# Weight loads moved from SP's queue to GpSimd's, and one split's low part made two turns later

## The chip, the cores and the metric

The kernel runs on one core of a Trainium2 chip. The time is the device time of one execution in microseconds. Three runs of the kernel before took 670.84, 672.91 and 673.17 us; the median is 672.91.

The engines that matter: PE (TensorE) multiplies matrices, DVE (VectorE) and ACT (ScalarE) work on elements, POOL (GpSimd) does a little set-up, and SP (SyncE) issues the DMAs. Each engine has a queue of its own that it works through in order. A DMA instruction in a queue waits there until its semaphores allow it, and what stands behind it waits too.

## The reference

Windowed attention with sink tokens, and then two MLPs, all in float32:

```
scores = q k^T / 8,   kept where key < 4 or 0 <= query - key < 128
x = softmax(scores) v                     (2 batches, 8 heads, 768 tokens, head size 64)
h = x @ w_in ;  g = max(h, 0) + alpha * min(h, 0) ;  y = g @ w_out    (1536 x 512, 512 x 2048)
h = y @ w2_in ; g = h - tanh(h) ;                    out = g @ w2_out
```

The weights arrive as 64-bit floats. [...]

## The kernel before

**Attention** goes in turns `n`, one for a pair of heads of one block of 128 tokens (96 turns; four make a block `u`). A turn's work on DVE is the mask and maximum (`s_max`, L279), the sum and its reciprocal (L294, L296), the scaling of the probabilities (`norm`, L303), and sometimes a copy of the sink columns (L309) and the differences that split a float into a high and a low part (`kq_lo` L237, `x_l` L374). PE makes the scores of the next turn (`s_mm`, L264 for the first block, L270 later), transposes the scaled probabilities (L319) and multiplies them by v (L358 to L362).

**The MLPs** go in 96 steps `g`: twice three groups of 512 tokens, each over 16 slices `f` of 128 hidden units. Every float32 operand of these matmuls is split into a high part of fewer bits and the remainder; three products are summed. `split_w` makes the high part of a weight tile on ACT (`wh`, L215), `split_lo` the low part on DVE (`wl`, L220). Part 0 of a slice feeds `h_mm` (L389), part 1 feeds `out_mm` (L441).

**Weights** come slice by slice. `load_w` (L194) issues two DMAs of 512 KB, L197 and L198, into one of two staging buffers. `conv_w` turns them into floats: two ACT instructions (L73, L74) and two DVE instructions (L76, L78), spread over steps. L78 is the last that reads the staging buffer, so the load of slice f+2 waits for L78 of slice f. There are 32 loads, 16 for each MLP.

**The order** is written out by hand: the program order of each engine is the order in which the Python code names its instructions (`manual_schedule`). The opening runs 19 turns (S_LEAD) of attention alone, `n` from 0 to 18, with the conversion of slice 0 begun in turn 8 and of slice 1 in turn 12 (CONV0). From then on each step of the first MLP carries one attention turn, until the turns are used up. During the first MLP's first token group each step also converts one slice of the first MLP's weights. The second MLP's weights are converted from the end of the second token group on.

SP issues nearly everything: the q and k loads (L180, four DMAs of 64 KB for each half block), v (L185), the sink rows (L188), the weights (L197, L198) and the results. In the opening POOL makes two iotas (L491, L492) and the identity matrix, and after that it has nothing to do. The masks of the attention are built by DVE from the iotas (L494 to L503).

The place that the change touches in the opening loop stands at the end of a turn, behind the conversions' own steps:

```
            for f, at in CONV0:                      # (0, 8), (1, 12)
                ...
                if at < n < at + 5:
                    conv_step(0, f)
                ...
                if n == at + 6 and f == 0:           # turn 14
                    split_w(0, 0, 0, 0)              # ACT, L215
                    split_lo(0, 0, 0, 0)             # DVE, L220
```

In turn 14 the loop comes to f = 0 first and to f = 1 after it, so the split of slice 0 stands ahead of L78 of slice 1 in DVE's queue.

Of the kernel before, what the change touches and what calls it, by code (L numbers as in the profile page):

```python
# [11 lines left out]
I32 = mybir.dt.int32  # L12
# [68 lines left out]
def load_scalars(nc, pool, limits):  # L81

    raw = pool.tile([128, 2, 2], I32, name="ns_raw")
    nc.sync.dma_start(out=raw.rearrange("p a t -> p (a t)"), in_=limits.bitcast(I32).partition_broadcast(128))
    val = pool.tile([128, 2], F32, name="ns_val")
    return raw, val
# [52 lines left out]
def fast_path(tc, qk, v, vsink, limits, w1i, w1o, alpha, w2i, w2o, out, outer):  # L139
    nc = tc.nc  # L140
    keep = outer.enter_context(tc.tile_pool(name="keep", bufs=1))
    bad_i = keep.tile([1, 1], I32, name="bad_i")
    with ExitStack() as ctx:
# [50 lines left out]
        def load_w(m, f):  # L194
            wi, wo = ((w1i, w1o), (w2i, w2o))[m]
            raw = stage[m][f % 2]
            nc.sync.dma_start(out=raw[:, 0:1024], in_=wi[f].rearrange("p k c -> p (k c)").bitcast(I32))  # L197
            nc.sync.dma_start(out=raw[:, 1024:2048], in_=wo[f * 128:(f + 1) * 128, :].bitcast(I32))  # L198

        def conv_w(m, f):  # L200
            raw = stage[m][f % 2]
# [9 lines left out]
        def split_w(m, c, f, part):  # L211
            src = wf[m, f][:, 512 * part:512 * part + 512]
            hi = wp.tile([128, 512], F32R, name=f"wh{part}", tag=f"wh{part}", bufs=2)
            lo = wp.tile([128, 512], F32R, name=f"wl{part}", tag=f"wl{part}", bufs=2)
            nc.scalar.activation(out=hi, in_=src, func=AF.Copy, scale=W_DOWN)  # L215
            whl[m, c, f, part] = (hi, lo)

        def split_lo(m, c, f, part):
            hi, lo = whl[m, c, f, part]
            nc.vector.scalar_tensor_tensor(lo, wf[m, f][:, 512 * part:512 * part + 512], W_DOWN, hi, op0=ALU.mult, op1=ALU.subtract)  # L220
# [34 lines left out]
        def s_mm(n):  # L255

            u, p, b, i, w = geom(n)
            for a in range(2):
                if (n, a) not in sps:
                    sps[n, a] = ps_tile(["o"] if initial[0] else ["st"[a]])  # L260
            if u == 0:
                for a in range(2):
                    t = raws[2 * u + p // 2][64 * a:64 * a + 64, p % 2]
                    nc.tensor.matmul(sps[n, a][:, :w], lhsT=t[:, 0, :], rhs=t[:, 1, :], start=True, stop=True)  # L264
                return
            at = 0 if u % 2 == 0 else K_ODD + 128
            for e, (l, r) in enumerate(((0, 0), (1, 0), (0, 1))):
                for a in range(2):
                    h = slice(64 * a, 64 * a + 64)
                    nc.tensor.matmul(sps[n, a][:, :w], lhsT=kq[l][h, p, at:at + 128], rhs=kq[r][h, p, K_EVEN:K_EVEN + w], start=e == 0, stop=e == 2)  # L270

        def s_max(n, a):
            u, p, b, i, w = geom(n)
            G, hh = 2 * u + p // 2, 2 * (p % 2) + a
            if hh == 0:
                pq[G] = ap.tile([128, 4, 288], F32, name="pq", bufs=2)
                sums[G] = ap.tile([128, 4], F32, name="sums", bufs=2)
            mask = m_zero if i == 0 else m_one if i == 1 else m_even if i % 2 == 0 else m_odd
            nc.vector.tensor_tensor_reduce(  # L279
                out=pq[G][:, hh, 0:w], in0=sps.pop((n, a))[:, :w], in1=mask[:, 0:w], scale=-0.125, scalar=BIG,  # L280
                op0=ALU.add, op1=ALU.min, accum_out=nm[:, 2 * n + a:2 * n + a + 1],
            )

        def s_exp(n, a):
            u, p, b, i, w = geom(n)
            G, hh = 2 * u + p // 2, 2 * (p % 2) + a
            e = pq[G][:, hh, 0:w]
            nc.scalar.activation(out=e, in_=e, func=AF.Exp, scale=-1.0, bias=nm[:, 2 * n + a:2 * n + a + 1], accum_out=sums[G][:, hh:hh + 1])  # L288

        def norm_sum(n, part):  # L290
            u, p, b, i, w = geom(n)
            r = sums[2 * u + p // 2][:, 2 * (p % 2):2 * (p % 2) + 2]
            if part == 0:
                nc.vector.tensor_scalar(r, r, 1e-9, None, op0=ALU.add)  # L294
            else:
                nc.vector.reciprocal(r, r)  # L296

        def norm(n):
            u, p, b, i, w = geom(n)
            G, hh = 2 * u + p // 2, 2 * (p % 2)  # L300
            for a in range(2):
                e = pq[G][:, hh + a, 0:w]
                nc.vector.tensor_scalar(e, e, sums[G][:, hh + a:hh + a + 1], None, op0=ALU.mult)  # L303
        def sink_copy(n):
            u, p, b, i, w = geom(n)
            G = 2 * u + p // 2
            if p % 2 == 1 and i >= 2:
                sks[G] = ap.tile([128, 4, SINK], F32, name="sk", bufs=1)
                nc.vector.tensor_copy(sks[G], pq[G][:, :, 128:160])  # L309

        def t_mm(n):
            u, p, b, i, w = geom(n)
            G, hh = 2 * u + p // 2, 2 * (p % 2)
            tps[n] = t = ps_tile(["t", "h"] if initial[0] else ["t"])
            cur = 0 if i % 2 == 0 else 160
            for a in range(2):
                for e, c in ((0, 160 - cur), (1, cur)):
                    if i > 0 or e == 1:
                        nc.tensor.transpose(t[:, 256 * a + 128 * e:256 * a + 128 * e + 128], pq[G][:, hh + a, c:c + 128], ident)  # L319

        def t_ev(n):
            u, p, b, i, w = geom(n)
            ptb[n] = ap.tile([128, 2, 2, 128], F32, name="pt", bufs=2)
            e0 = 1 if i == 0 else 0
            tv = tps.pop(n).rearrange("p (a e c) -> p a e c", a=2, e=2)
            nc.scalar.activation(out=ptb[n][:, :, e0:, :], in_=tv[:, :, e0:, :], func=AF.Copy)  # L326

        def has_sinks(n):
            u, p, b, i, w = geom(n)
            return p % 2 == 1 and i >= 2  # L330
# [12 lines left out]
        def sink_ev(n):  # L343
            pts[n // 2] = ap.tile([128, 128], F32, name="pts", bufs=2)
            nc.scalar.activation(out=pts[n // 2], in_=tps.pop((n, 0))[:, 384:512], func=AF.Copy)
# [123 lines left out]
        raw, val = load_scalars(nc, const, limits)  # L469
# [50 lines left out]
        def a_loads(n):  # L520

            u, p = divmod(n, 4)
            if p == 3 and 2 <= u + 1 < NU:
                load_v(u + 1)
            if n % 2 == 0 and 6 <= n // 2 + 4 < 2 * NU:
                load_qk(n // 2 + 4)
            if n == 4 * NB + 4:
                load_vs(1)


        def splits_hi(n):

            for G in {0: (0, 2), 1: (1,)}.get(n, (n // 2 + 2,) if n % 2 != (n < S_LEAD - 1) else ()):
                if G < 2 * NU:
                    kq_hi(G)
# [20 lines left out]
        for n in range(S_LEAD):  # L556
            last = n == S_LEAD - 1
            a_loads(n)
            if n == 0:
                s_mm(0)  # L560
            if not last:
                s_mm(n + 1)
            if n >= 2:
                t_ev(n - 2)
            s_max(n, 0)
            s_max(n, 1)
            s_exp(n, 0)
            s_exp(n, 1)
            if n >= 2 and has_sinks(n - 2):
                sink_ev(n - 2)  # L570
            if n >= 1:
                norm_sum(n - 1, 0)
                norm_sum(n - 1, 1)
                norm(n - 1)
                sink_copy(n - 1)
                if not last:
                    t_mm(n - 1)
                    if has_sinks(n - 1):
                        sink_mm(n - 1, n + 1)
            if n >= 2 and not last:  # L580
                pv(n - 2)
            splits_hi(n)
            if n >= 5 and n % 4 == 1:
                x_h(n - 2)
            splits_lo(n)
            if n >= 5 and n % 4 == 2:
                x_l(n - 3)
            if n == 1:
                masks(0)
            if n == 4:  # L590
                masks(1)
            if n == 3:
                load_w(0, 1)
            for f, at in CONV0:
                if n == at:
                    conv_start(0, f)
                if at < n < at + 5:
                    conv_step(0, f)
                if n == at + 4:
                    load_w(0, f + 2)  # L600
                if n == at + 6 and f == 0:
                    split_w(0, 0, 0, 0)
                    split_lo(0, 0, 0, 0)
        initial[0] = False
        conv_start(0, len(CONV0))
# [41 lines left out]
        for g in range(N):  # L647
            m, c, f = steps[g]
            n = S_LEAD + g
# [332 lines left out]
```

## Time and profile before

| | |
|---|---|
| median of 3 runs | 672.91 us |
| profiled execution, its own time | 672.6 us |
| its span in the profile | 670.8 us |
| PE busy | 640.8 us (96%), 3194 matmuls |
| DVE busy | 526.4 us (78%) |
| ACT busy | 472.5 us (70%) |
| POOL busy | 1.1 us, 8 instructions |
| mean DMA rate | 71 GB/s over the span |

The span runs from the first to the last instruction. Busy PE is matmuls in flight, whose ends are modelled. A row of the timeline gives the start in us, the duration (of a row that merges several instructions, the whole), the engine, the line of the kernel, the operation, the tiles (out<-in), and in brackets how long the engine had stood idle and what released it. `SPq` is SP's queue of DMA issues. The granted clock is a share of PE's full 2.4 GHz: 1.00 is that, 0.50 is 1.2 GHz.

### The profile page before, as it was taken

To read this page: it belongs to the slowest core of one execution; us is meant where nothing else is said; L and a number is where in the kernel's file an instruction comes from. 1 tells how busy PE (TensorE), PEld (TensorE's weight loads), DVE (VectorE), ACT (ScalarE), POOL (GpSimd) and SP (SyncE) were. 2 spreads that over 40 slices of the span, in tenths; PEclk is the share of its full clock that TensorE was granted. 3 is DMA by queue.
4 is the path that set the end of the run, shared out by engine and by line. 5 is a ranking of instruction groups with operands and counts; after the bars stand their busy time and mean duration, and the time that the engine had idled before them with its cause. 6 is when DMAs were issued, how large, how long until landed. Compare 5 with 4: busy or idle time off the path is not lost.

```text
span 670.8 us, 9201 instructions
## 1 busy us (share of the span) xinstructions
PE 640.8 (96%) x3194; PEld 504.2 (75%) x3194; DVE 526.4 (78%) x1098; ACT 472.5 (70%) x936; POOL 1.1 (0%) x8
## 2 busy tenths in 40 slices
PE   5886999999999999999899999999999999999996
PEld 3564677777777777777787887887888888888884
DVE  6877889799576665548877777889998888888883
ACT  5876888787566564557766757877877777777763
POOL 0000000000000000000000000000000000000000
PEclk9978899999999999999999999999999999999999
DMA  6543444463010000203343420100010000100001
GB/s 160 189 136 98 142 157 150 162 222 111 0 48 17 1 16 1 95 33 143 119 177 127 152 99 1 63 1 0 1 63 1 2 0 1 63 1 0 1 1 68
DMA packets 27032, 47.36 MB, mean 71 GB/s; under 512 B 3168, under 2 KB 15456, under 8 KB 26976
## 3 DMA queue, kind: packets, MB, share of 16 engines
q1 hardware_dynamic: 26400, 46.42, 20.0%
q8 instruction: 27, 0.44, 0.3%
q10 hardware_dynamic: 576, 0.26, 0.2%
q14 instruction: 29, 0.24, 0.1%
HBM read 43.53 MB, written 3.15 MB: 70 GB/s over the span
## 4 chain that ended last, share of the span: by engine, by line
PE 77%; ACT 8%; DVE 8%; issue 2%; DMA 2%; SPq 1%; ACTq 0%; DVEq 0%
PE ps_o L441 33%; PE ps_h L389 21%; PE ps_s L389 7%; PE ps_t L389 6%; ACT wf L73 2%; PE ps_t L319 2%; PE ps_s L270 2%; DMA raw<-in_moe_w_out_dram 2%; ACT raw L74 2%; PE ps_v L358 2%; PE ps_v L362 2%; PE ps_v L359 1%; PE ps_o L270 1%; DVE wf L78 1%; ACT pq L288 1%
## 5 line engine op out<-in xcount | busy, mean ns | idle before, releaser
L220 DVE SCALAR_TENSOR_TENSOR wl<-wf,wh 128x512 fp32r<-128x512 f32 x192 | 123.4, 683 | 44.7 <-ACT wh L215 44.7
L389 PE MATMUL ps_h<-x,wh 128*128 128x512 f32 x384 | 124.5, 405 | 2.1 <-ACT t L396 1.9
L215 ACT ACTIVATE wh<-wf 128x512 fp32r<-128x512 f32 x192 | 110.9, 628 | 5.1 <-PE ps_o L441 5.0
L389 PEld LDWEIGHTS ps_h<-x,wh 128*128 128x128 f32 x384 | 68.7, 189 | 18.2 <-ACT t L396 3.1
L441 PE MATMUL ps_o<-gh,wh 128*128 128x512 f32 x192 | 76.6, 399 | 0.3 <-DVE y L452 0.3
L389 PE MATMUL ps_h<-x,wl 128*128 128x512 f32 x192 | 75.8, 395 | 0.0
L441 PE MATMUL ps_o<-wh,gh 128*128 128x512 f32 x192 | 74.8, 390 | 0.2 <-ACT gh L420 0.2
L441 PE MATMUL ps_o<-gh,wl 128*128 128x512 f32 x192 | 74.9, 390 | 0.0
L441 PE MATMUL ps_o<-gl,wh 128*128 128x512 f32 x192 | 74.8, 390 | 0.0
L441 PE MATMUL ps_o<-wh,gl 128*128 128x512 f32 x192 | 74.8, 390 | 0.0
L441 PE MATMUL ps_o<-wl,gh 128*128 128x512 f32 x192 | 74.7, 389 | 0.0
L288 ACT ACTIVATE pq<-pq,nm 128x288 f32<-128x288 f32 (+1 forms) x96 | 48.4, 506 | 30.2 <-DVE nm L279 29.8
L420 ACT ACTIVATE gh<-g 128x512 fp32r<-128x512 f32 x48 | 30.4, 633 | 36.5 <-DVE g L127 36.5
L76 DVE SCALAR_TENSOR_TENSOR wf<-wf,raw 128x1024 int32<-128x1024 int32 x32 | 39.1, 1221 | 19.0 <-ACT raw L74 19.0
L326 ACT ACTIVATE pt<-ps_t 128x512 f32<-128x512 f32 (+1 forms) x39 | 21.9, 562 | 35.5 <-PE ps_t L319 35.4
L441 PEld LDWEIGHTS ps_o<-gh,wh 128*128 128x128 f32 x192 | 36.1, 188 | 9.2 <-issue 1.4
L420 ACT ACTIVATE gh<-t 128x512 fp32r<-128x512 f32 x48 | 30.1, 627 | 18.2 <-DVE t L408 18.2
L389 PEld LDWEIGHTS ps_h<-x,wl 128*128 128x128 f32 x192 | 36.2, 188 | 7.9
L441 PEld LDWEIGHTS ps_o<-wh,gh 128*128 128x128 f32 x192 | 36.0, 188 | 8.0 <-ACT gh L420 0.6
L441 PEld LDWEIGHTS ps_o<-wh,gl 128*128 128x128 f32 x192 | 36.0, 188 | 7.9 <-DVE gl L425 0.4
L441 PEld LDWEIGHTS ps_o<-gh,wl 128*128 128x128 f32 x192 | 36.0, 188 | 7.8
L73 ACT ACTIVATE wf<-raw 128x1024 f32<-128x1024 f32 x32 | 36.6, 1143 | 7.4 <-DMA raw<-in_moe_w_out_dram 7.3
(145 smaller groups left out, 1290.6 us busy)
## 6 DMA issues: line engine op xcount, KB each, us to landing
raw<-in_moe_w_in_dram SPq DMA_DIRECT2D x32, 512.0 KB, 3.3
raw<-in_moe_w_out_dram SPq DMA_DIRECT2D x32, 512.0 KB, 4.2
raw_qk<-in_qk_dram SPq DMA_DIRECT2D x92, 64.0 KB, 3.0
vt<-in_v_dram SPq DMA_DIRECT2D x12, 256.0 KB, 3.1
out_dram<-ob SPq DMA_DIRECT2D x2, 1024.0 KB, 4.2
out_dram<-ob SPq DMA_DIRECT2D x4, 256.0 KB, 3.4
vs<-in_vsink_dram SPq DMA_DIRECT2D x2, 256.0 KB, 3.6
raw_qk<-in_qk_dram ACTq DMA_DIRECT2D x4, 64.0 KB, 2.7
```

Of the source, the lines that this page charges most:

```text
L73: nc.scalar.activation(out=dst, in_=hw.bitcast(F32), func=AF.Abs, scale=W_UP, accum_out=seen)
L74: nc.scalar.activation(out=lw, in_=top, func=AF.Copy, scale=1.0 / 8192, bias=FLOOR)
L76: nc.vector.scalar_tensor_tensor(di, di, 3, lw, op0=ALU.logical_shift_left, op1=ALU.bitwise_or)
L215: nc.scalar.activation(out=hi, in_=src, func=AF.Copy, scale=W_DOWN)
L220: nc.vector.scalar_tensor_tensor(lo, wf[m, f][:, 512 * part:512 * part + 512], W_DOWN, hi, op0=ALU.mult, op1=ALU.subtract)
L270: nc.tensor.matmul(sps[n, a][:, :w], lhsT=kq[l][h, p, at:at + 128], rhs=kq[r][h, p, K_EVEN:K_EVEN + w], start=e == 0, stop=e == 2)
L288: nc.scalar.activation(out=e, in_=e, func=AF.Exp, scale=-1.0, bias=nm[:, 2 * n + a:2 * n + a + 1], accum_out=sums[G][:, hh:hh + 1])
L319: nc.tensor.transpose(t[:, 256 * a + 128 * e:256 * a + 128 * e + 128], pq[G][:, hh + a, c:c + 128], ident)
L326: nc.scalar.activation(out=ptb[n][:, :, e0:, :], in_=tv[:, :, e0:, :], func=AF.Copy)
L389: nc.tensor.matmul(h_ps[f], lhsT=l[:, w], rhs=x[:, r, kk, :], start=kk == 0 and e == 0, stop=kk == 3 and e == 2)
L420: nc.scalar.activation(out=gh, in_=mid[f], func=AF.Copy)
L441: nc.tensor.matmul(o, lhsT=l, rhs=r, start=f == 0 and e == 0, stop=f == NF - 1 and e == 2)
```

## The change

It has two parts. `load_w` issues both DMAs of each of the 32 loads on GpSimd's queue instead of SP's. And in the opening the low part of the first split (slice 0, part 0) is made at the end of turn 16, two turns behind its high part, which stays in turn 14.

```diff
             raw = stage[m][f % 2]
-            nc.sync.dma_start(out=raw[:, 0:1024], in_=wi[f].rearrange("p k c -> p (k c)").bitcast(I32))
-            nc.sync.dma_start(out=raw[:, 1024:2048], in_=wo[f * 128:(f + 1) * 128, :].bitcast(I32))
+            nc.gpsimd.dma_start(out=raw[:, 0:1024], in_=wi[f].rearrange("p k c -> p (k c)").bitcast(I32))
+            nc.gpsimd.dma_start(out=raw[:, 1024:2048], in_=wo[f * 128:(f + 1) * 128, :].bitcast(I32))
...
                 if n == at + 6 and f == 0:
                     split_w(0, 0, 0, 0)
+                if n == at + 8 and f == 0:
                     split_lo(0, 0, 0, 0)
```

On DVE, the end of turn 14 and the first maximum of turn 15 (`x` is the attention's output, `wl` the low part, `wf` a weight slice in conversion, `pq` the scores), before:

```order
L309 COPY sk<-pq 128x128
L374 TENSOR_TENSOR x<-ps_v,x 128x4x128
L220 SCALAR_TENSOR_TENSOR wl_649<-wf,wh_648 128x512
L78 SCALAR_TENSOR_TENSOR wf<-raw_90,wf 128x1024
L279 ISA pq,nm<-ps_o,m_odd 128x288
```

And the same place in the change, followed by the end of turn 16:

```order
L309 COPY sk<-pq 128x128
L374 TENSOR_TENSOR x<-ps_v,x 128x4x128
L78 SCALAR_TENSOR_TENSOR wf<-raw_90,wf 128x1024
L279 ISA pq,nm<-ps_o,m_odd 128x288
...
L303 TENSOR_SCALAR pq<-pq,sums 128x288 x2
L309 COPY sk<-pq 128x128
L220 SCALAR_TENSOR_TENSOR wl_649<-wf,wh_648 128x512
L279 ISA pq,nm<-ps_o,m_even 128x288
```

L220 has moved from ahead of L78 and the maxima of turn 15 to behind turn 16's copy of the sink columns and ahead of the maxima of turn 17.

On POOL, the start of the kernel, before:

```order
L977 UNCONDITIONAL_BRANCH
L491 ISA
L491 IOTA rel_i 128x128
L492 IOTA col_i 128x128
masks.py:197 MEMSET ident 128x128
masks.py:199 AFFINE_SELECT ident<-ident 128x128
L134 TENSOR_LOAD bad_i
```

And in the change:

```order
L978 UNCONDITIONAL_BRANCH
L197 DMA raw_90<-in_moe_w_in_dram 128x1024
L198 DMA raw_90<-in_moe_w_out_dram 128x1024
L491 ISA
L491 IOTA rel_i 128x128
L492 IOTA col_i 128x128
masks.py:197 MEMSET ident 128x128
masks.py:199 AFFINE_SELECT ident<-ident 128x128
L197 DMA raw_90<-in_moe_w_in_dram 128x1024
L198 DMA raw_90<-in_moe_w_out_dram 128x1024
```

The first load's two issues stand ahead of the iotas, the second's directly behind the identity matrix; the 30 other loads follow, with nothing between them.

On SP, the start of the kernel, before:

```order
L84 DMA ns_raw<-in_limits_dram 128x4
L180 DMA raw_qk<-in_qk_dram 64x2x128 x8
L185 DMA vt<-in_v_dram 128x512 x2
L180 DMA raw_qk<-in_qk_dram 64x2x128 x8
L188 DMA vs<-in_vsink_dram 128x512
L197 DMA raw_90<-in_moe_w_in_dram 128x1024
L198 DMA raw_90<-in_moe_w_out_dram 128x1024
L180 DMA raw_qk<-in_qk_dram 64x2x128 x4
L485 DMA al<-in_moe_alpha_dram 128x16
L197 DMA raw_90<-in_moe_w_in_dram 128x1024
L198 DMA raw_90<-in_moe_w_out_dram 128x1024
```

And in the change:

```order
L84 DMA ns_raw<-in_limits_dram 128x4
L180 DMA raw_qk<-in_qk_dram 64x2x128 x8
L185 DMA vt<-in_v_dram 128x512 x2
L180 DMA raw_qk<-in_qk_dram 64x2x128 x8
L188 DMA vs<-in_vsink_dram 128x512
L180 DMA raw_qk<-in_qk_dram 64x2x128 x4
L485 DMA al<-in_moe_alpha_dram 128x16
```

The weight loads are gone from SP's queue, and the rest keeps its order. PE's and ACT's instructions keep theirs.

## Rows read from the trace of the kernel before

**Rows 1.** Busy time by stretch: length, then PE, PEld, DVE, ACT, POOL, clock, DMA share, GB/s.

```profile
102.00:150.00 48.00, 47.14 (x256) 35.25 (x256) 42.63 (x100) 39.46 (x86) 0.00 (x0) 1.00 0.53 185
...
300.00:400.00 100.00, 97.78 (x435) 79.70 (x435) 77.48 (x102) 69.63 (x115) 0.00 (x0) 1.00 0.38 137
```

**Rows 2.** Timeline of turn 14: start, duration, engine, line, operation, idle time before and releaser.

```profile
48.97 0.66 PE L270 MATMUL ps_o<-kq 64*128 64x288 f32 x6
...
49.19 0.62 ACT L215 ACTIVATE wh<-wf 128x512 fp32r<-128x512 f32 x1
...
49.84 0.69 DVE L220 SCALAR_TENSOR_TENSOR wl<-wf,wh 128x512 fp32r<-128x512 f32 x1 [1.19 <-ACT wh L215]
...
50.45 1.22 DVE L78 SCALAR_TENSOR_TENSOR wf<-raw,wf 128x1024 int32<-128x1024 int32 x1
...
51.59 0.45 DVE L279 CUSTOM_DVE_ANT_0 pq<-ps_o,m_odd 128x288 f32<-128x288 f32 x1
...
53.25 0.82 PE L319 MATMUL ps_h<-ident,pq 128*128 128x128 f32 x4 [3.63 <-DVE pq L303]
```

**Rows 3.** Timeline of turn 16, PE's score matmuls and DVE's first maximum of turn 17.

```profile
56.22 0.98 PE L270 MATMUL ps_o<-kq 64*128 64x288 f32 x6
...
57.24 0.46 DVE L279 CUSTOM_DVE_ANT_0 pq<-ps_o,m_even 128x288 f32<-128x288 f32 x1 [1.28 <-PE ps_o L270]
```

**Rows 4.** Busy time by stretch, two microseconds within turns 15 and 16.

```profile
54.00:56.00 2.00, 2.00 (x13) 1.66 (x12) 1.86 (x9) 1.63 (x5) 0.00 (x0) 0.50 1.00 390
```

**Rows 5.** Waits of SP's own queue: total, times, longest.

```profile
SPq L197 <- DVE wf L78: 192.1, 28, 29.6
```

**Rows 6.** Weight loads: issue to landing of their tile, then from the page's DMA issues.

```profile
DMA to landing us min/median/max: 3.1/4.1/6.4
...
raw<-in_moe_w_out_dram SPq DMA_DIRECT2D x32, 512.0 KB, 4.2
```

**Rows 7.** Timeline: issues of weight loads on SP, and ACT's first reading of them.

```profile
78.41 0.43 SPq L198 DMA_DIRECT2D raw<-in_moe_w_out_dram  x1
...
83.13 1.14 ACT L73 ACTIVATE wf<-raw 128x1024 f32<-128x1024 f32 x1
...
122.12 1.16 ACT L73 ACTIVATE wf<-raw 128x1024 f32<-128x1024 f32 x1 [1.20 <-DMA raw<-in_moe_w_out_dram]
...
153.28 0.43 SPq L198 DMA_DIRECT2D raw<-in_moe_w_out_dram  x1
...
159.63 1.17 ACT L73 ACTIVATE wf<-raw 128x1024 f32<-128x1024 f32 x1
```

**Rows 8.** Timeline of PE: the first output matmul of four steps.

```profile
119.97 0.40 PE L441 MATMUL ps_o<-gh,wh 128*128 128x512 f32 x1
...
127.63 0.39 PE L441 MATMUL ps_o<-gh,wh 128*128 128x512 f32 x1
...
142.50 0.40 PE L441 MATMUL ps_o<-gh,wh 128*128 128x512 f32 x1
...
149.76 0.39 PE L441 MATMUL ps_o<-gh,wh 128*128 128x512 f32 x1
```

**Rows 9.** Timeline of the opening.

```profile
1.11 0.23 DVE L494 CAST rel<-rel_i 128x128 f32<-128x128 int32 x1
...
5.11 1.89 PE L264 MATMUL ps_o<-raw_qk 64*128 64x128 f32 x8 [5.11 <-DMA raw_qk<-in_qk_dram]
...
5.91 0.29 DVE L279 CUSTOM_DVE_ANT_0 pq<-ps_o,m_zero 128x128 f32<-128x128 f32 x1 [0.35 <-PE ps_o L264]
...
13.45 0.43 SPq L197 DMA_DIRECT2D raw<-in_moe_w_in_dram  x1
```

**Rows 10.** Busy time by stretch, two stretches of the opening.

```profile
2.00:4.00 2.00, 0.00 (x0) 0.00 (x0) 0.58 (x4) 0.23 (x2) 0.00 (x0) 1.00 0.72 118
...
16.00:18.00 2.00, 2.00 (x14) 1.23 (x12) 1.93 (x14) 1.72 (x7) 0.00 (x0) 1.00 1.00 398
```

**Rows 11.** Timeline of DVE, 0.3 us behind a conversion's last instruction.

```profile
115.96 0.48 DVE L303 TENSOR_SCALAR pq<-pq,sums 128x128 f32<-128x128 f32 x2
```

## The prediction

> **What bounds the kernel now.** I read the stretches first. In the first MLP's opening pass, where attention, weight conversion and matmuls run together, PE is busy 47.1 of 48 us, but DVE is busy 42.6 and ACT 39.5 [rows 1]: DVE has 11% of the stretch left, ACT 18%. There the work that feeds PE has little air. In the stretch from 300 us on, where the second MLP's weights are converted, PE is busy 97.8 of 100 us and DVE 77.5 [rows 1]: PE alone sets the pace. Second I read the timeline of the one place where the moved split stands, turn 14 [rows 2]; third, SP's own waits and the landings of the weight loads [rows 5 to 7]; last, the first microseconds [rows 9, 10].
>
> **Part 1, the low part two turns later.** In turn 14 DVE is free at 48.65 us but waits 1.19 us for ACT to finish the high part, then spends 0.61 us on the low part until the next instruction starts at 50.45, and only then comes L78 and, at 51.59, the score maximum of the next turn [rows 2]. PE meanwhile stands 3.63 us for the normalised scores that come behind this maximum [rows 2]. With the low part gone, L78 starts at 48.65, takes its 1.14 us (50.45 to 51.59), and the maximum can start at 49.79: the scores that it reads are written by PE at 48.97 + 0.66 = 49.63, so they are just there, and the next thing that would be late is nothing before 49.79. Gain 51.59 − 49.79 = 1.80 us, and PE's idle time falls from 3.63 to 1.83.
> What is put back two turns on costs 0.61 us of DVE. It stands between turn 16's copy of the sink columns and turn 17's first maximum, where DVE waits 1.28 us for PE's scores [rows 3]; 0.61 fits inside, and the high part is then long written, so there is no wait in it. If PE's scores came 0.7 us earlier there, the cover would be gone and 0.61 would count. The first user of the low part is the first MLP's first matmul, after turn 18. So I take −1.8, with bounds −1.2 (cover gone) and −3.1. The −3.1 is the clock: from 54 us on PE's granted clock is 0.50, which is the lower level, 1.2 GHz [rows 4], and the six score matmuls take 0.98 us there against 0.66 before the idle stretch [rows 2, 3]. Should the shorter idle stretch leave the clock at its upper level, the 3.95 us of PE between 53.25 and the maximum's start at 57.24 less its 0.04 shrink by a third, 1.3 us. I do not count it, since 1.83 us of idle time remain.
>
> **Part 2, the weight queue.** What it removes from SP: 64 issues of some 0.4 us (0.43 in the rows) and their waits. But the waits at L197 are for DVE's L78 in 28 of the 32 loads, 192.1 us in all [rows 5]: the queue waited because the staging buffer was still being read, and GpSimd's queue will wait for the same L78. No weight load can start earlier in the steady part. The q, k and v loads behind them on SP go earlier, yet no engine waits for one of those after the first at 5.11 us [rows 9]. So the gain is 0.
> What it adds: POOL issues instead of SP, and no row of this trace shows a POOL issue. The bounds for how much later a pair of loads lands: 0 (as on SP), and 2.3 us, the longest landing of a weight load less the median, 6.4 − 4.1 [rows 6]. I take 1.0, nearer the lower, because the 1.05 MB of a pair take 2.6 us at the 398 GB/s of a stretch with full engines [rows 10], and this part of a landing is the same for any issuer. The Trainium skill ("DMA: Bandwidth & Descriptors", section "Specifications") gives the first byte of a GpSimd-issued transfer at about 1 us against about 0.6 from SP; no run here shows it, and by it the lateness would be about 0.4, the sum 0.8 us lower in the next paragraph.
> What 1.0 us later costs: between 78 and 160 us there are eleven loads; the first is issued at 78.41, lands 4.2 us on at 82.6 and is read by ACT at 83.13, the last lands at 157.5 and is read at 159.63 [rows 6, 7]. Taken one by one, their slack is 0.5, 0.1, 2.2, 0.1, 1.5, none, 2.7, none, 0.4, 0.9 and 2.1 us; one without slack is the 1.20 us wait at 122.12 [rows 7]. One more microsecond makes ACT wait 0.5 + 0.9 + 0.9 + 1.0 + 1.0 + 0.6 + 0.1 = 5.0 us more. How much of an ACT wait reaches PE: the step that holds the 1.20 us wait lasts 127.63 − 119.97 = 7.66 us, a later one without a wait 149.76 − 142.50 = 7.26 [rows 8]; 0.4 of 1.2 is a third. I take 0.4 of each, with 0 and 1 as bounds: 2.0 us. At 2.3 us of lateness the same list gives 15.2 us of waiting and 6.1 us of time. In the second MLP's conversions PE is nearly full [rows 1] and hides such waits; only where the last token group begins do ACT's evictions gate PE, and there I put 0.5 (0 to 2).
>
> **Part 3, the opening.** Nothing holds the first two weight pairs on POOL, so 2 MB that SP issued from 13.45 us on [rows 9] now start at about 1 us, with the q and k loads on which PE's first matmul waits until 5.11 [rows 9]. The DMA engines are 0.72 busy there [rows 10]. A pair needs 2.6 us of full engines. Between 2 and 6 us there is room for 0.28 × 4 = 1.1 us of it; 1.5 us are too many, and q and k bear perhaps two thirds: +1.0. The bounds are 0 (all of it lands behind q and k) and 2.6. Also, the iotas behind which DVE's cast at 1.11 us starts now stand behind the first two weight issues; the masks are needed at 5.91 [rows 9], so this runs beside the q, k wait unless POOL takes more than a microsecond for each. A shift here reaches the end, since everything behind it is chained.
>
> **Sum.** −1.8 + 1.0 + 2.0 + 0.5 = +1.7 us on the profiled execution's 672.6 (span 670.8 and 1.8 around it), which is 0.3 under the median of 672.91: 674.3 us. Half a per cent, 3.4 us, is about what a measurement of this kernel can tell from no change.
>
> **Rivals.**
> *DVE and POOL shut each other out (slower).* Right behind L78, at 115.96, DVE runs its short normalisations of SBUF data [rows 11], just when the queue that waited for L78 issues. If DVE's op cannot run while POOL prepares a pair, it is held for up to two issues, at SP's price 2 × 0.43 = 0.86 us [rows 7]. DVE has 11% left there, so 0.89 of it counts: 11 × 0.77 = 8.4 us, in place of the 2.0 + 0.5. 672.6 − 1.8 + 1.0 + 8.4 = 680.2. It turns the result slower by over half a per cent once the hold exceeds 0.43 us a load. For it: DVE is the fullest engine behind PE. Against it: in the opening POOL's small ops and DVE's cast run together, 0.23 us for the cast [rows 9], with no visible stretch. The Trainium skill ("SBUF — State Buffer", section "Who interferes with whom") states such an exclusion between GpSimd and those DVE ops that use two ports, and that it starves GpSimd-issued DMAs. By it the lock could also fall the other way, on the load, which is the late landing above.
> *The opening collides (slower).* Both pairs, 5.2 us of full engines, fall before the early q, k and v loads, and the masks come late too: +4 instead of +1.0, 677.3. For it: 0.72 is already in use. Against: the second pair goes out only behind the iotas.
> *The queue change is free and the clock stays up (faster).* −3.1 and nothing else: 669.5. For it: SP's 0.43 us may be close to POOL's. Against: a transfer of 2.6 us is added to a busy stretch.
> *It does not do what it says.* SP's queue frees nothing that anyone waits for; this is already in the forecast, and alone would be −1.8: 670.8.
>
> **How the numbers follow.** The forecast (around 674.3, its own range 671 to 678) gets 0.43: of that 0.35 within half a per cent, 0.07 slower, 0.01 faster. DVE against POOL 0.22, all slower. The colliding opening 0.12: 0.07 slower, 0.05 same. The free queue, with or without the clock, 0.23: 0.11 faster, 0.12 same. Together 0.12 faster, 0.52 same, 0.36 slower. The range that leaves out 2 in 10 runs from 669.8 to 680.5.
>
> **What would show it.** Right: in turn 14 L78 directly behind the x difference, and PE's idle time near 1.8 instead of 3.63; low part beside PE's scores in turn 16; more ACT waits for the weight loads than 1.20 us at a time; PE's first matmul after 6 us. Wrong: the first matmul still at 5.1; DVE's normalisations behind L78 longer than 0.48 us for two (the rival); PE's clock at its upper level from 51 to 57 us; weight loads that land in 4.2 us or less.

## The result and the profile after

The changed kernel takes 676.44 us (median of 8 runs, 673.22 to 678.08); the kernel before took 672.08 beside it (8 runs, 670.7 to 673.51). The ratio is 1.0064, 95% interval 1.0049 to 1.0078: slower by 0.64%, 4.4 us. The profiled execution of the changed kernel took 678.08 us (span 676.3), the longest of its eight. Its last matmul stands 4.6 us later than in the profile of before, and another 0.9 us lies behind the last work, where the results go out. I account for the 4.6.

From the timelines I took each turn's reciprocal (L296), and after the opening each step's first output matmul (L441), and set them against before:

| place | offset to before, us |
|---|---|
| turn 0 | +4.07 |
| turn 13 | +3.85 |
| turn 14, behind the moved split | +1.97 |
| turn 16 | +0.89 |
| turn 20 | +0.13 |
| first MLP, first step (81.2 us) | +0.08 |
| third step (96.7), fourth step (104.9) | +0.49, +3.06 |
| end of its opening pass (165.1) | +3.53 |
| last token group's start (318.2) | +4.93 |
| 407.9 and to the last matmul | +4.6 |

So the opening loses 4 us, and turns 14 to 20 win them back: 1.88 at the split, 1.08 and 0.75 behind it, where the clock had fallen before. Then the first MLP's opening pass loses 3.5 and the boundary between the token groups 1.4.

**Opening.** The timeline of the changed kernel (columns as in [rows 2]) answers to [rows 9]:

```profile
1.20 8.21 SPq L180 DMA_DIRECT2D raw_qk<-in_qk_dram  x8
1.27 0.66 POOL L197 DMA_DIRECT2D raw<-in_moe_w_in_dram  x1 [0.82 <-POOLq L970]
1.93 0.53 POOL L198 DMA_DIRECT2D raw<-in_moe_w_out_dram  x1
...
2.83 0.38 DVE L494 CAST rel<-rel_i 128x128 f32<-128x128 int32 x1 [1.83 <-POOL rel_i L491]
...
3.45 0.55 POOL L197 DMA_DIRECT2D raw<-in_moe_w_in_dram  x1
...
5.41 0.20 DVE L503 TENSOR_SCALAR m_zero<-m_zero 128x128 bf16<-128x128 bf16 x1
...
8.23 0.76 PE L264 MATMUL ps_o<-raw_qk 64*128 64x128 f32 x2 [8.23 <-DMA raw_qk<-in_qk_dram]
9.03 0.29 DVE L279 CUSTOM_DVE_ANT_0 pq<-ps_o,m_zero 128x128 f32<-128x128 f32 x1 [3.43 <-PE ps_o L264]
```

The first matmul starts at 8.23 instead of 5.11, and its bracket names the q, k load. The masks are ready at 5.41 + 0.20 = 5.61, 3.4 us before the first maximum. SP needs 8.21 us for its first eight q, k issues; the same row of before shows 5.28:

```profile
1.19 5.28 SPq L180 DMA_DIRECT2D raw_qk<-in_qk_dram  x8
```

The stretches of the changed kernel (columns of [rows 1]) show why, against 0.72 and 118 GB/s in [rows 10]:

```profile
2.00:4.00 2.00, 0.00 (x0) 0.00 (x0) 0.98 (x6) 0.24 (x2) 1.84 (x7) 1.00 0.79 99
4.00:6.00 2.00, 0.00 (x0) 0.00 (x0) 1.46 (x7) 0.00 (x0) 0.52 (x1) 1.00 1.02 385
6.00:8.00 2.00, 0.00 (x0) 0.00 (x0) 0.00 (x0) 0.00 (x0) 0.00 (x0) 1.00 0.99 337
...
54.00:56.00 2.00, 0.77 (x8) 0.61 (x10) 1.93 (x10) 1.40 (x7) 1.05 (x2) 1.00 0.57 137
...
104.00:106.00 2.00, 1.40 (x7) 1.19 (x8) 1.72 (x6) 2.00 (x7) 0.00 (x0) 0.73 0.92 354
106.00:108.00 2.00, 2.00 (x6) 1.52 (x6) 2.00 (x5) 0.93 (x3) 0.00 (x0) 0.50 0.33 133
```

From 4 to 8 us the DMA engines are full (1.02, 0.99), and no compute engine but DVE with its masks has work.

**Turns 14 to 16.** Timeline of the changed kernel, answering to [rows 2, 3]:

```profile
51.82 0.68 DVE L374 TENSOR_TENSOR x<-ps_v,x 128x512 fp32r<-128x512 f32 x1
...
52.42 1.22 DVE L78 SCALAR_TENSOR_TENSOR wf<-raw,wf 128x1024 int32<-128x1024 int32 x1
...
53.56 0.45 DVE L279 CUSTOM_DVE_ANT_0 pq<-ps_o,m_odd 128x288 f32<-128x288 f32 x1
...
55.23 0.64 PE L319 MATMUL ps_h<-ident,pq 128*128 128x128 f32 x4 [1.76 <-DVE pq L303]
...
57.03 0.66 PE L270 MATMUL ps_o<-kq 64*128 64x288 f32 x6
...
57.86 0.68 DVE L220 SCALAR_TENSOR_TENSOR wl<-wf,wh 128x512 fp32r<-128x512 f32 x1
...
58.46 0.45 DVE L279 CUSTOM_DVE_ANT_0 pq<-ps_o,m_even 128x288 f32<-128x288 f32 x1
```

L78 stands right behind the x difference, and PE's idle time is 1.76 us instead of 3.63. The granted clock is 1.00 at 54 to 56 us, where it was 0.50 [rows 4]; turn 16's six score matmuls take 0.66 instead of 0.98. In turn 16 the low part has no cover left. PE's scores are written at 57.03 + 0.66 = 57.69, DVE's copy runs until L220 starts at 57.86, and the low part then holds the maximum until 58.46: its 0.60 us count, where L279 had 1.28 us of idle time before [rows 3].

**The steady part.** ACT's waits for weights, from the waits of the changed kernel (total, times, longest), and of before:

```profile
ACT wf L73 <- DMA raw<-in_moe_w_out_dram: 11.7, 9, 2.9
```

```profile
ACT wf L73 <- DMA raw<-in_moe_w_out_dram: 7.3, 6, 2.3
```

From issue to landing (last number, the median) the changed kernel's page has 3.6 and 4.3 us:

```profile
raw<-in_moe_w_in_dram POOLq DMA_DIRECT2D x32, 512.0 KB, 3.6
raw<-in_moe_w_out_dram POOLq DMA_DIRECT2D x32, 512.0 KB, 4.3
```

Before it was 4.2 for w_out [rows 6], and for w_in:

```profile
raw<-in_moe_w_in_dram SPq DMA_DIRECT2D x32, 512.0 KB, 3.3
```

GpSimd also starts later. At the last token group's start, changed kernel:

```profile
312.11 1.22 DVE L78 SCALAR_TENSOR_TENSOR wf<-raw,wf 128x1024 int32<-128x1024 int32 x1
313.87 0.53 POOL L197 DMA_DIRECT2D raw<-in_moe_w_in_dram  x1 [3.33 <-DVE wf L78]
314.39 0.53 POOL L198 DMA_DIRECT2D raw<-in_moe_w_out_dram  x1
314.44 1.12 ACT L73 ACTIVATE wf<-raw 128x1024 f32<-128x1024 f32 x1 [2.90 <-DMA raw<-in_moe_w_out_dram]
...
319.76 0.74 PE L389 MATMUL ps_h<-x,wh 128*128 128x512 f32 x2 [1.28 <-ACT t L396]
```

and before:

```profile
303.82 1.23 DVE L78 SCALAR_TENSOR_TENSOR wf<-raw,wf 128x1024 int32<-128x1024 int32 x1
305.12 0.33 SPq L197 DMA_DIRECT2D raw<-in_moe_w_in_dram  x1
...
309.52 1.12 ACT L73 ACTIVATE wf<-raw 128x1024 f32<-128x1024 f32 x1 [1.51 <-DMA raw<-in_moe_w_out_dram]
```

L78 ends at 313.33 and POOL's first issue is on record 0.54 us later, at 313.87; on SP it was 305.05 and 305.12, 0.07. An issue takes 0.53 instead of 0.33 to 0.43. ACT waits 2.90 us for the next load in place of 1.51, and PE then stands for ACT.

The largest single loss is one step of the first MLP, 97.22 to 107.91 (changed kernel):

```profile
97.22 0.39 PE L441 MATMUL ps_o<-gh,wh 128*128 128x512 f32 x1
...
101.29 1.14 ACT L73 ACTIVATE wf<-raw 128x1024 f32<-128x1024 f32 x1 [1.18 <-DMA raw<-in_moe_w_out_dram]
...
103.98 0.57 ACT L326 ACTIVATE pt<-ps_t 128x512 f32<-128x512 f32 x1
...
104.60 0.32 PE L270 MATMUL ps_t<-kq 64*128 64x128 f32 x1 [1.68 <-ACT pt L326]
...
105.18 1.22 PE L389 MATMUL ps_h<-x,wh 128*128 128x512 f32 x2
...
107.91 0.58 PE L441 MATMUL ps_o<-gh,wh 128*128 128x512 f32 x1
```

ACT comes to L73 late by 1.18 us, its eviction L326 stands behind it, PE idles 1.68 us for that, and then the granted clock is 0.73 and 0.50 (rows of the stretches above). The step lasts 10.69 us; before it lasted 104.85 − 96.73 = 8.12.

### The profile page after: what moved, and what is told of

Read it like the earlier page. It is cut to its first block, busy times and chain, and to the rows that moved or that the text cites. A ratio compares the mean times of both kernels' runs of the same rounds, so it can differ in the third digit from the quotient of the medians.

```text
span 676.3 us, 9240 instructions
## 1 busy us (share of the span) xinstructions
PE 639.9 (95%) x3194; PEld 503.5 (74%) x3194; DVE 526.8 (78%) x1098; ACT 472.6 (70%) x936; POOL 35.0 (5%) x72
## 3 DMA queue, kind: packets, MB, share of 16 engines
q0 software_dynamic: 9216, 33.56, 13.6%
## 4 chain that ended last, share of the span: by engine, by line
PE 81%; DVE 8%; ACT 6%; issue 2%; DMA 2%; SPq 0%; DVEq 0%; ACTq 0%
PE ps_o L441 35%; PE ps_h L389 23%; PE ps_s L389 6%; PE ps_t L389 6%; PE ps_t L319 2%; PE ps_s L270 2%; PE ps_v L358 2%; PE ps_v L359 1%; PE ps_v L362 1%; DVE pq L279 1%; ACT wf L73 1%; ACT raw L74 1%; DVE wf L76 1%; DMA raw_qk<-in_qk_dram 1%; PE ps_o L270 1%
## 5 line engine op out<-in xcount | busy, mean ns | idle before, releaser
L220 DVE SCALAR_TENSOR_TENSOR wl<-wf,wh 128x512 fp32r<-128x512 f32 x192 | 123.6, 684 | 43.4 <-ACT wh L215 43.4
L441 PE MATMUL ps_o<-gh,wh 128*128 128x512 f32 x192 | 76.8, 400 | 0.3 <-DVE y L452 0.3
L441 PE MATMUL ps_o<-wh,gh 128*128 128x512 f32 x192 | 74.8, 390 | 0.2 <-ACT gh L420 0.2
L441 PE MATMUL ps_o<-gh,wl 128*128 128x512 f32 x192 | 74.9, 390 | 0.0
L441 PE MATMUL ps_o<-gl,wh 128*128 128x512 f32 x192 | 74.8, 390 | 0.0
L441 PE MATMUL ps_o<-wh,gl 128*128 128x512 f32 x192 | 74.8, 390 | 0.0
L441 PE MATMUL ps_o<-wl,gh 128*128 128x512 f32 x192 | 74.7, 389 | 0.0
L326 ACT ACTIVATE pt<-ps_t 128x512 f32<-128x512 f32 (+1 forms) x39 | 21.8, 559 | 36.2 <-PE ps_t L319 36.1
L73 ACT ACTIVATE wf<-raw 128x1024 f32<-128x1024 f32 x32 | 36.5, 1142 | 11.8 <-DMA raw<-in_moe_w_out_dram 11.7
L441 PEld LDWEIGHTS ps_o<-gh,wh 128*128 128x128 f32 x192 | 36.2, 189 | 9.2 <-issue 1.4
L441 PEld LDWEIGHTS ps_o<-wh,gh 128*128 128x128 f32 x192 | 36.0, 188 | 8.1 <-ACT gh L420 0.6
L441 PEld LDWEIGHTS ps_o<-wh,gl 128*128 128x128 f32 x192 | 36.0, 188 | 7.9 <-DVE gl L425 0.4
L441 PEld LDWEIGHTS ps_o<-gh,wl 128*128 128x128 f32 x192 | 36.0, 188 | 7.8
```

What stands on the lines that cost most here:

```text
L73: nc.scalar.activation(out=dst, in_=hw.bitcast(F32), func=AF.Abs, scale=W_UP, accum_out=seen)
L441: nc.tensor.matmul(o, lhsT=l, rhs=r, start=f == 0 and e == 0, stop=f == NF - 1 and e == 2)
```

## The experiments

They were timed in three sets on three chips (the first four below, the next four, the last two), each beside the kernel before, whose medians were 671.5, 671.7 and 671.3. Prices are differences of medians; taken from the ratios instead they differ by up to 1.4 us, most where two sets are compared. Diffs are against the changed kernel.

**The split alone** (both issues of `load_w` back to `nc.sync`):

> Only the low part is moved; all weight loads stay on SP. Theory A (the shorter idle stretch of PE in turn 14 keeps the clock up): 1.9 us from turn 14, 1.1 from the turn-16 matmuls at full clock and 0.75 from the stretch near 66 to 70 us, so about 3.7 under the kernel before: 668.4 against 672.1; granted clock 1.00 from 51 to 58 us, PE's idle time before the transposes of turn 14's scores about 1.8. Rival B (the clock stayed up in the changed kernel only because its opening began 4 us later): 1.9 under, 670.2, and the clock again at 0.50 behind that idle time.

Measured 667.94 us (666.24 to 669.22), ratio 0.9936, interval 0.9917 to 0.9955. A's time came, and this is the best version: it beats both kernels. A's reason did not come: A wanted the clock at 1.00 from 51 to 58 us, and it fell at 52, as B said, a little sooner than before. In the profile (span 667.4) the reciprocals are 3.31 us ahead at turn 20. Of this 0.68 was there at turn 13 already, ahead of the moved instruction; 1.88 came at turn 14, near the computed 1.80; 0.75 came between turns 19 and 20. The clock in three stretches (columns of [rows 1]):

```profile
52.00:54.00 2.00, 2.00 (x10) 1.51 (x10) 1.90 (x8) 1.16 (x6) 0.00 (x0) 0.50 1.01 377
54.00:56.00 2.00, 2.00 (x17) 1.48 (x17) 1.06 (x7) 1.30 (x3) 0.00 (x0) 0.68 0.21 47
66.00:68.00 2.00, 2.00 (x17) 1.54 (x12) 1.90 (x6) 2.00 (x4) 0.00 (x0) 1.00 0.08 25
```

**The queue alone**:

```diff
-                if n == at + 8 and f == 0:
                     split_lo(0, 0, 0, 0)      # under n == at + 6 again
```

> Only the queue is changed; high and low part of the first split stay together in turn 14. Theory A (the terms add): the changed kernel's 676.4 plus the 3.7 us of the split, 680.1, some 8 over the kernel before. Rival C (the loss in the opening is soaked up by slack later on, so the split's gain would not have been needed to make it good): no more than 677.

Measured 679.7 us, ratio 1.0108 (1.0083 to 1.0133), as A said. The parts add up: −3.6 and +8.2 to +4.6, measured +4.4.

**The first two pairs back on SP:**

```diff
+            engine = nc.sync if m == 0 and f < 2 else nc.gpsimd
-            nc.gpsimd.dma_start(...)   # both
+            engine.dma_start(...)
```

> The changed kernel, but the first two weight pairs are issued by SP at their old places; the other thirty by GpSimd. Theory A (2 MB of weights ahead of the first q and k loads cost the opening 4.1 us, of which 3.85 last): 676.4 - 3.85 = 672.6, first matmul at 5.1 us again. Rival C (soaked up later): 676.4.

Measured 671.82 us, ratio 0.9998 (0.9982 to 1.0015): A. The opening is as before; against the split alone, the first pass is 1.56 us longer (85.41 against 83.85, from first step to eleventh behind it) and the boundary 1.3. The other thirty loads cost 671.82 − 667.94 = 3.9 by the medians.

**Only the first two pairs on GpSimd** (`nc.sync if m == 1 or f >= 2 else nc.gpsimd`):

> The low part is moved; only the first two weight pairs are issued by GpSimd, the other thirty by SP. Theory A (terms add): split alone plus 3.85, about 672.3, first matmul at 8.2 us; the steps behind 80 us as in the kernel before, ACT's waits for weight loads 7.3 us in all as there. Rival D (GpSimd's queue costs through the thirty later loads, and the opening's loss fades): near the split alone, 668.4.

Measured 672.54 us, ratio 1.0013 (0.9997 to 1.0029): A. 672.54 − 667.94 = 4.6 us for these two pairs. The first matmul comes at 8.19, and everything behind the opening goes as before (first pass 83.64 us).

**The first pair behind the iotas** (`load_w(0, 0)` moved below `make_identity`):

> The changed kernel with the first weight pair issued by GpSimd behind the iotas and the identity matrix, so that the masks are as early as before. Theory A (the opening's 4.1 us are DMA traffic ahead of q and k): no relief, 676 to 677, first matmul still behind 8 us. Rival E (the late iotas and masks cost it): about 672.5, first matmul near 5.1 us.

Measured 676.93 us, ratio 1.0084 (1.0056 to 1.0113): A. The masks' cast is back at 1.11 us and nothing is won:

```profile
1.11 0.23 DVE L494 CAST rel<-rel_i 128x128 f32<-128x128 int32 x1
1.80 0.67 POOL L197 DMA_DIRECT2D raw<-in_moe_w_in_dram  x1
...
8.34 0.76 PE L264 MATMUL ps_o<-raw_qk 64*128 64x128 f32 x2 [8.34 <-DMA raw_qk<-in_qk_dram]
```

So the late masks cost nothing; as PE's bracket says, the opening waits for the q and k transfers.

**Only the very first pair on GpSimd** (`nc.sync if m == 1 or f > 0 else nc.gpsimd`):

> The low part is moved; only the very first weight pair is issued by GpSimd, the others by SP. Theory A (each megabyte ahead of q and k costs its 2.6 us of full engines, less what room there is): half of the opening's loss, 1.5 to 2.5 us over the split alone, 669.4 to 670.4; first matmul between 6 and 7 us. Rival I (the first pair alone does the damage, since q and k for the first matmul are issued before the second pair): all 4.1, 672.0, first matmul at 8.2 us.

Measured 670.95 us, ratio 0.9992 (0.9978 to 1.0007). Neither: the time lies between theory A and rival I, and the first matmul is at 8.24, as rival I said. Turn 0 is 2.81 us late against 4.07 with two pairs, and the median is 3.0 us above the split alone. One pair holds the first matmul as long as two do; the second adds some 1.3 us to the turn.

```profile
8.24 1.39 PE L265 MATMUL ps_o<-raw_qk 64*128 64x128 f32 x8 [8.24 <-DMA raw_qk<-in_qk_dram]
```

**A small part of each load back on SP,** so that SP waits for L78 again and the q, k loads behind it are not issued in one bunch (the kernel with the first two pairs on SP, and):

```diff
-            engine.dma_start(out=raw[:, 1024:2048], in_=...)
+            engine.dma_start(out=raw[:, 1024:1984], in_=src[:, 0:960])
+            nc.sync.dma_start(out=raw[:, 1984:2048], in_=src[:, 960:1024])
```

> As the run with the first two pairs on SP, but of each later load SP issues the last 64 of 1024 columns of the output weights, so that SP's queue again waits for L78 at every load and the q, k and v loads behind it go out as in the kernel before, while 97% of the weights stay on GpSimd's queue. Theory F (in the first MLP's opening pass a weight pair lands late because eight q and k loads, no longer held back, run beside it): no pair lands later than 6 us behind its issue, where 8.1 was seen, and the steps between 78 and 160 us lose under 0.8 us against the split alone; second token group's end still 1.4; about 670. Rival G (each pair is late by GpSimd's own issue alone): the steps lose 1.5 or more as without the pacing; 671.8.

Measured 672.06 us, ratio 1.0013 (0.9999 to 1.0027). Theory F falls, and the figures are rival G's: a landing of 6.4 us is still there, and the first pass is 85.97 us, 2.1 longer than with the split alone. That the bunched q, k loads cause the pass's loss isn't shown by anything here.

**Only the second MLP's loads on GpSimd** (`nc.sync if m == 0 else nc.gpsimd`):

> The low part is moved; only the second MLP's sixteen loads are issued by GpSimd, when all q, k and v loads are long done. Theory A (a pair lands some 0.7 us later, and only the start of the third token group feels it): split alone plus 1.4, 669.3; ACT waits 2.9 us instead of 1.5 at the second of these conversions, PE 1.3 us more at the group's start, all other steps of 5.44 us unchanged. Rival H (PE hides the whole of the second MLP's loading): 667.9.

Measured 670.89 us (668.41 to 675.08), ratio 0.9987 (0.9969 to 1.0006). Above both: 2.9 us over the split alone by the medians, though its profile (span 669.4 against 667.4) shows 0.8 at the boundary and 0.3 later, and steps of 5.44 us as ever. I can place only 1.1 of it.

**The second half of a load later by GpSimd's own hand** (the kernel with the first two pairs on SP, and between its two issues):

```diff
+            if m == 0 and f >= 2:
+                for _ in range(6):
+                    nc.gpsimd.iota(idle_i, pattern=[[1, 128]], base=0, channel_multiplier=0)
```

> The kernel with the first two weight pairs back on SP's queue and the other thirty on GpSimd's (671.82 us, ratio to the kernel before 0.9998), and six idle iotas of 128x128 on GpSimd between the two issues of each of the first MLP's fourteen later loads, so that the second half of such a pair is issued about 1.1 us later (six times 0.18, from the starts of the iotas in the opening). Theory L (the loads cost time because they land late and ACT's conversions wait): fourteen times up to 1.1 us more of waiting, of which a third to a half reaches PE: ACT's waits for the weights grow by 6 to 12 us in all, and the time by 2 to 5 us: 674 to 677, ratio 1.003 to 1.007. Theory T (they cost time because of the traffic beside them, and not because of their lateness): 671.8 within 0.8 us, ratio 0.999 to 1.001, with ACT's waits no longer by more than 3 us.

Measured 676.48 us, ratio 1.0088 (1.0067 to 1.0109): +4.7, in L's direction, with the time at the upper end of L's range and the ratio above it. The dose was larger than meant, 1.8 us:

```profile
80.21 0.60 POOL L199 DMA_DIRECT2D raw<-in_moe_w_in_dram  x1 [4.14 <-issue]
80.81 1.79 POOL L202 IOTA idle_i<- 128x128 int32 x6
82.60 0.55 POOL L203 DMA_DIRECT2D raw<-in_moe_w_out_dram  x1
```

The first pass takes 88.48 us, and in it ACT waits 10.2 us for weights (8 times) against 4.1 (5 times) without the iotas and 1.9 (2 times) with the split alone. So 6.1 us of waiting cost 3.07 us of time: landing later is enough to make a loss in this pass.

**The two halves on two queues** (w_in on GpSimd, w_out on SP, first two pairs on SP):

> The same kernel with the pairs' first halves (w_in) on GpSimd's queue for thirty loads and all second halves (w_out) on SP's queue, each behind the same wait for L78: the two issues run side by side, the second no later than in the kernel with all loads on SP. Theory L (lateness of the pair's landing is what costs): w_in is issued 0.5 us later than from SP but w_out not later, so a pair lands 0 to 0.3 us later: 668 to 669.5, ratio 0.994 to 0.997, ACT's waits for weights under 9 us. Theory T (that GpSimd issues at all, or that the loads are not in line with q and k, is what costs): 670.5 to 672, ratio 0.998 to 1.000.

Measured 671.4 us (668.78 to 674.47), ratio 0.9996 (0.9979 to 1.0013). By the time this is T, and L's figure was missed; ACT's waits were 10.7 us instead of under 9. The profiled execution (668.8, second fastest of twelve) says otherwise for its own part: the first pass takes 83.76 us, no loss, and the boundary loses 0.5 instead of 1.3 (both against the split alone). L's premise failed as well: the pairs landed no earlier. In the pass w_in, now the later half, lands 5.9 us behind the end of L78 (median), against 5.4 for the pair with both halves on GpSimd and 4.7 with both on SP. Among the twelve, five with a mean granted clock under 0.99 took 671.5 to 674.5, the seven others 668.8 to 671.5; the split alone had no such execution in six. So part of what GpSimd's queue costs may come as more frequent clock falls, which one profile doesn't show. This is left open.

Why 1.8 us more of waiting than with the split alone (3.7 against 1.9) cost nothing here, while 2.2 us more cost 1.56 with the first two pairs on SP, the steps of the pass show. For each step: its length without a wait, then ACT's wait for weights in it and how much longer the step was.

| step | no wait, us | wait → longer by, us |
|---|---|---|
| first | 7.48 | 0.32 → 0.39 (changed kernel); 0.77 → 0.81 (first pair behind the iotas); 1.01 → 1.06 (first two pairs on SP); 1.26 → 1.20 (six iotas) |
| fourth | 7.96 | 0.89 → 0 (first two pairs on SP); 1.30 → 0 (two queues); 1.70 → 0.02 (small part on SP); 2.01 → 0.25 (six iotas) |
| eighth | 7.03 (waits to 0.74) | 0.89 → 0.02 (two queues); 1.22 → 0.06 (queue alone); 1.70 → 0.54 (first two pairs on SP); 2.21 → 1.00 (small part on SP); 3.05 → 1.82 (six iotas) |

A wait costs what exceeds its step's own room: nothing is free in the first step, some 1.7 us in the fourth, some 1.2 in the eighth. With the first two pairs on SP, 1.06 + 0.54 make up the pass's 1.56:

```profile
80.86 1.18 ACT L73 ACTIVATE wf<-raw 128x1024 f32<-128x1024 f32 x1 [1.01 <-DMA raw<-in_moe_w_out_dram]
...
135.80 1.15 ACT L73 ACTIVATE wf<-raw 128x1024 f32<-128x1024 f32 x1 [1.70 <-DMA raw<-in_moe_w_out_dram]
```

With the halves on two queues every wait fell within its step's room; the longest stands in the fourth step:

```profile
102.42 1.17 ACT L73 ACTIVATE wf<-raw 128x1024 f32<-128x1024 f32 x1 [1.30 <-DMA raw<-in_moe_w_in_dram]
```

So lateness accounts for the pass in both.

## Why the prediction was right or wrong

The time, 676.44, lies inside the range, 2.1 us above the forecast; the sign was right, and the outcome, slower by just over half a per cent, was given 0.36 beside 0.52 for no change. The change itself was forecast at +1.7 and measured at +4.4. That the time came this near is luck: the split was taken 1.8 us too small, the opening 3.6 and the thirty later loads 1.4 too small with the opposite sign, and the kernel before came out 0.8 us faster in these eight runs than in the three that the forecast set out from. The rival "the opening collides", 677.3, was nearer.

- **The split, −1.8: right at turn 14, too small in all.** L78 came right behind L374, PE idled 1.76 us (1.83 forecast), and the turns gained 1.88, as they did, to 0.05 us, in all ten profiles that have the split moved. The cover in turn 16 was taken to hold, with "cover gone" and "the clock stays up" as opposite bounds. In the changed kernel both came together: with the clock up PE's scores were early, the low part's 0.60 us counted, and turn 16 still gained 1.08 in all. By medians the split is worth 3.6, twice the forecast. What failed is "I do not count it": in the profile of the changed kernel the clock stayed up at 54 to 56 us (−1.08) and again near 66 (−0.75; 0.80 and 0.50 before, 1.00 after). That the shorter idle stretch of PE kept it up isn't shown. The −1.08 stands in five of the ten profiles and the −0.75 in seven; in the split alone the clock fell at 52 us all the same, and 0.68 of its gain came ahead of turn 14, where a fall from 32 to 44 us before lasted only from 38 to 42. So what the split is worth beyond 1.88 us, and why, stays open.
- **The opening, +1.0 with 0 to 2.6: wrong, +4.1 at turn 0 and 4.6 by the medians.** The step that failed is "1.5 us are too many, and q and k bear perhaps two thirds". I shared the DMA engines' time by bytes and let the small loads get their part. In fact one pair alone puts the first matmul from 5.1 to 8.2 us, 3.1 us, more than the whole 2.6 us that I had put down for its transfer. SP's issues stretch too: in the changed kernel its sixth q, k issue starts at 5.99 us, right behind the landing, at 5.98, of its first. The DMA engines took about one packet of the one kind for one of the other (last section), and a weight packet is the larger by far. This is the size of the rival "the opening collides", though not by its whole mechanism: the masks were in time, and the second pair, issued behind the iotas, added some 1.3 us to turn 0 and nothing to the first matmul.
- **Lateness 1.0, first pass +2.0: right in kind, the price per wait misread.** ACT's waits in the pass grew, and with more lateness the loss grew. GpSimd adds 0.47 us before a pair's first issue (0.54 against 0.07), 0.1 to 0.2 by that issue's length before the second, and 0.1 in the second's landing: about 0.7 to 0.8 in all. With the 1.8 us of the iotas on top the pass lost 88.48 − 83.85 = 4.6 us, without them 1.6. The pass cost 1.2 to 1.6 us in the kernels without a clock fall in it (85.12 and 85.41 against 83.85), 3.45 in the profiled execution with one. The 0.4 of each wait came from comparing two different steps [rows 8]. The step that holds the 1.20 us wait, the sixth, lasts 7.64 to 7.66 us also in the profiles where ACT waits there for 0.2 us or less; what the wait adds is 0.15 us to the step behind it (7.85 against 7.70). So there is no fixed share: the half that the iotas give (3.07 / 6.1) is a mean over steps with more and less room. The list of slacks gave 5.0 us of new waits and gives 3.4 for 0.75 us of lateness; 2.0 to 2.2 came, and why the rest did not isn't shown. For 0.4 us of lateness the same list gives 1.4 us of waiting and 0.6 of time, so the sum would have been 1.4 us lower, not 0.8.
- **The boundary, +0.5 with 0 to 2: in its bounds, +1.4** here and 1.3 in the kernels that keep those loads on GpSimd.
- **"No engine waits" for SP's freed loads, gain 0: not contradicted.** No step of the first pass became shorter by more than 0.2 us when q, k and v went earlier.
- **DVE and POOL shutting each other out: refuted as a price on DVE.** Behind L78 the two normalisations take 0.65 us beside an issue, as elsewhere:

```profile
102.22 0.65 DVE L303 TENSOR_SCALAR pq<-pq,sums 128x288 f32<-128x288 f32 x2
...
102.45 0.54 POOL L197 DMA_DIRECT2D raw<-in_moe_w_in_dram  x1 [8.79 <-issue]
```

  Nor does the hold fall on the issue: in 27 of the 28 loads that waited for L78 the first issue is on record 0.54 or 0.55 us behind L78's end, whatever DVE runs then.

Added up by experiments: split −3.6, first two pairs +4.6, thirty later loads +3.9: +4.9 against +4.4 measured, within the uncertainty of the medians.

## What to carry to other kernels

A wait in a busy DMA queue can be what keeps large loads behind the small ones that the start needs; before a load is moved to an idle queue, ask what it would then be issued beside, and price that at the whole transfer and not at a share of it. An issuer that starts half a microsecond later makes every reload late, and a late reload costs what exceeds the room of the step that feels it, from nothing to the whole wait. Read that room by setting the same step with and without a wait side by side, not two different steps. Two edits in one change should be timed apart: here one is worth −3.6 us and the other +8.

## What the runs showed that I had not expected

- One early pair of 512 KB loads holds 64 KB loads issued at the same time: first matmul 5.11 to 8.24 us with one pair, 8.19 to 8.34 with two. The page shows the packets of the two kinds (queue: packets, MB, share of 16 engines):

```profile
q0 software_dynamic: 9216, 33.56, 13.6%
q1 hardware_dynamic: 17184, 12.86, 6.3%
```

  The weights go in packets of 33.56 MB / 9216 = 3.6 KB, the rest in 0.75 KB on average. Among the packets of the changed kernel's trace that start from 4.5 to 5.0 us, 41 are of 4096 B on the weights' queue and 45 of 512 B on SP's: about one for one, so that eight bytes of weights went for each byte of q and k.
- Six iotas between two issues took 1.79 us, 0.30 each, where two in the opening follow each other at 0.18.
- The clock's falls come and go with small shifts of the turns. By stretches of 2 us it is under 0.95 at 32 to 44, 52 to 58 and 66 to 72 us before; at 38 to 42 and 52 to 56 with the split alone; at 36 to 48 and 104 to 110 in the changed kernel; at 36 to 42 alone with the halves on two queues. A single profile prices a term only to some 2 to 3 us (668.8 against a median of 671.4 with the halves on two queues); the medians of four to twelve runs were needed.
